# A fused attention and gated-feed-forward block on one core: K products behind the first group's h, tile 1 transposed first, bias as a full transpose

## The chip, the cores and the metric

The kernel runs on one core of one Trainium2 chip. The metric is device time in microseconds (us). A core has five engines that run their own instruction streams and wait for each other on semaphores: TensorE (PE) for matrix products, VectorE (DVE), ScalarE (ACT), GpSimd (POOL), and SyncE (SP), which here only issues DMA transfers. Products land in PSUM, eight banks of 128 x 512 float32, and have to be read out by DVE or ACT before a bank can be used again.

## The reference

The input x has 2048 tokens of 448 features, in bfloat16. All else works on its layer norm xn.

```
xn = (x - mean) / sqrt(var + 1e-5)
q, k, v = xn @ wqkv                       # 16 heads of 28
phi(t) = where(t > 0, t + 1, exp(t)) + 1e-6
kv = phi(k)^T v ;  z = sum over tokens of phi(k)
s = (phi(q) kv / (phi(q) z + 1e-6)) @ wo
h = relu(xn @ w1 + b1)^2                  # 1792 hidden features
out = x + s * silu(h @ w2 + b2)
```

## The kernel before

**Tiles and groups.** Tokens are cut into 16 tiles of 128 (`si`), four tiles to a group (`g`, 0 to 3). The 448 features are contracted in three chunks of 128 rows and a remainder of 64 rows. The hidden features of h are 14 blocks of 128 (`fi`), named H0 to H13. Per group there are three Q products of 512 tokens (Q0 to Q2), per tile one K product (K0 to K15, 448 columns). v is never formed; its weights are folded in later.

**Who sets the order.** Every step is recorded by `add` as an operation of an engine, with the tiles that it reads and writes, an estimated cost and sometimes a priority. `Program.place` then runs a model of the chip. The streams of PE and SP keep the order in which the steps are written. ACT, DVE and POOL take, among what is ready, the operation that the model wants first; some operations may go to either of two engines (`alts`), and the model chooses. Each product's buffer (`Buf`) gets the PSUM bank that the model sees free first. `Program.emit` writes out the streams with the waits that follow from all this; an operation's waits stand ahead of its first instruction. A written order on PE is therefore kept exactly, and every other engine's order, the choice of engine and the banks may move when one line moves.

**The start, tiles 0 to 3.** SP issues the loads of x and of the weights one after another. `ln_stats`, `ln_rstd` and `ln_norm` make the layer norm of a tile: DVE takes the statistics (L418, L421), ACT the root by Ln and Exp (L426, L430), DVE writes xn (L436). `ln_twin` (L448) copies the 64 features of the remainder beside themselves, since they are used from both halves of the rows. `warm` feeds PE products of ones until data is there. `tile_transpose` transposes three chunks of a tile on PE (L479) into two banks and copies them out to `xT` on ACT or DVE (L487). The first six h blocks of group 0, `heads`, are built while tiles come in: `h_part(si, c)` (L1007) adds chunk c of tile si to all six banks as one operation of six products; `h_rests` (L1022) closes them with the 64-row remainder. `b1_rows` turns the bias of h, loaded as 14 rows of 128, into columns by a transpose on PE (L1038) and a copy on ACT.

**Bursts.** After that PE works mostly in bursts of four products (`fours`), named by a text such as "Q0 Q1|Q2 H3'"; a prime means the next group. The two products left of the bar begin in the lower 64 rows of the array, the two on the right in the upper, at the same time; a burst is four operations: the first four steps of the first left and first right product, the same for the second two, and then the last three steps of each. Each operation waits for its banks as a whole.

**Evictions.** An h block is emptied by a relu with bias (L603 on ACT; two of the heads go to DVE, L600) and squared in SBUF (DVE L609 or ACT L610). A K or Q product goes through `phi`: ACT writes its exponential (L539), DVE takes min(e, 1) + 1e-6 in SBUF (L544), and then the larger of that and the product plus one, reading PSUM (L549). Only this last one sets the bank free. For each K after the first, POOL then adds the tile's result into `zacc` (L573).

**Later.** Groups 1 to 3 get their layer norm in `ln_group`, and xT by a DMA transpose that SP issues for two tiles at a time (L464). `gates` multiplies h by w2 for two tiles (L874), with a burst of the next group between its halves. The end brings the sum over tokens, the denominator, and out.

Of the kernel before, what the change touches and what calls it, by code (L numbers as in the profile page):

```python
# [9 lines left out]
P = 128  # L10
S, D, F = 2048, 448, 1792
NT, NG, NF = S // 128, S // 512, F // 128
# [24 lines left out]
class Program:  # L37
# [9 lines left out]
    def add(self, eng, emit, reads=(), writes=(), dur=0.2, alts=(), nbytes=0, mode=None, after=(), prio=None, lead=0.0):  # L47
        op = Op(eng, emit, reads, writes, {eng: dur, **dict(alts)}, mode, nbytes, after)
        for t in op.reads:
            w = self.writer.get(t)  # L50
            if w is not None:
                op.deps.add(w)
            self.readers.setdefault(t, []).append(op)
        for t in op.writes:
            w = self.writer.get(t)
            if w is not None and w is not op:
                op.deps.add(w)
            for r in self.readers.get(t, ()):
                if r is not op:
                    op.deps.add(r)  # L60
            self.writer[t] = op
            self.readers[t] = [r for r in self.readers.get(t, ()) if r is op]
        op.deps.discard(op)
        for d in op.deps:
            d.succ.append(op)
        op.prio, op.lead = prio, lead
        self.ops.append(op)
        return op
# [174 lines left out]
def bass_recurrent_scan__linear_attn_block__dense_activation_squared_relu__prompt_kernel(  # L243
    nc, A_x, A_wqkv, A_wo, B_x, B_w1, B_b1, B_w2, B_b2, out
):
    with ExitStack() as es:
        sb = lambda name, shape, dtype: es.enter_context(nc.sbuf_tensor(name, shape, dtype))
# [14 lines left out]
        w_1 = sb("w_1", [P, 4, F], bf)  # L262
        w_2 = sb("w_2", [P, NF, D], bf)
        w_o = sb("w_o", [P, 7, D], bf)
        b1r = sb("b1r", [NF, P], bf)
        b1f = sb("b1f", [P, NF], f32)
        b2b = sb("b2b", [P, D], bf)
        st6 = sb("st6", [P, NT, 6], f32)
# [28 lines left out]
        def pool(fn, writes, reads=(), dur=0.25, prio=None):  # L297
            return add("pool", fn, reads, writes, dur, prio=prio)

        pool(lambda e, _: e.memset(ident[:, :], 0.0), ["ident"], dur=0.14, prio=-9)  # L300
        pool(
            lambda e, _: e.affine_select(
# [39 lines left out]
        def dma(eng, dst, src, writes, nbytes, reads=(), after=(), prio=None, rate=None):  # L342
            return add(
                eng, lambda e, _: e.dma_start(dst, src), reads, writes, 0.45 if eng == "sp" else 0.5, nbytes=nbytes,  # L344
                after=after, prio=prio, mode=rate or 270e3,
            )

        def load_x(lo, hi, rate=None):
            dma(
                "sp", x_tok[:, lo:hi, :], x_r[:, lo // 4, lo % 4 : lo % 4 + hi - lo, :], [("x", i) for i in range(lo, hi)], (hi - lo) * P * D * 2,  # L350
                rate=rate,
            )

        def load_main(w, src, name, lo, hi):
            dma(
                "sp", w[:, 0:3, lo:hi], src[0:384, lo:hi].rearrange("(c p) j -> p c j", p=P), [(name, "m")],
                768 * (hi - lo),
            )
# [8 lines left out]
                rate=rate,  # L367
            )

        dma("act", b1r[:, :], B_b1.rearrange("(f p) -> f p", p=P), ["b1r"], F * 2, prio=-8.5)  # L370
        load_x(0, 1)
        load_x(1, 2, rate=250e3)
        load_x(2, 4, rate=300e3)
# [6 lines left out]
        for h in (0, 1):  # L380
            src = B_w1[384:448, 768:1792].rearrange("p (b j) -> p b j", j=256)[:, h::2, :]
            dst = w_1[HALF[h], 3, 768:1792].rearrange("p (b j) -> p b j", j=256)[:, h::2, :]
            dma("sp", dst, src, [("w1r", h)], 128 * 512)
        load_main(w_1, B_w1, "w1c", 1280, 1792)
        load_x(4, 8)
        load_main(w_qkv, A_wqkv, "wk", D, 2 * D)
        load_rest("sp", w_qkv, A_wqkv, "wqk", 0, 0, 2 * D)
        load_rest("sp", w_qkv, A_wqkv, "wqk", 1, 0, 2 * D)
# [27 lines left out]
        def ln_stats(si, prio=None, after=()):  # L416
            add(
                "dve", lambda e, _: e.bn_stats(st6[:, si, :], x_tok[:, si, :]), [("x", si)], [("st", si)], 0.53 if prio is None else 0.63,  # L418
                prio=prio, after=after,
            )  # L420
            add("dve", lambda e, _: e.bn_aggr(mv[:, si, :], st6[:, si, :]), [("st", si)], [("mv", si)], 0.07, prio=prio and (0.0, 0.3, 0.3, -0.5, 2.7)[prio])  # L421

        def ln_rstd(lo, hi, prio=None):
            c = slice(lo, hi)
            add(
                "act", lambda e, _: e.activation(out=rstd[:, c], in_=mv[:, c, 1], func=AF.Ln, bias=eps5[:, 0:1]),  # L426
                [("mv", i) for i in range(lo, hi)] + ["eps5", "actw"], [("ve", i) for i in range(lo, hi)], 0.19, prio=prio,
            )
            add(
                "act", lambda e, _: e.activation(out=rstd[:, c], in_=rstd[:, c], func=AF.Exp, scale=-0.5),  # L430
                [("ve", i) for i in range(lo, hi)], [("rstd", i) for i in range(lo, hi)], 0.13, prio=prio,
            )

        def ln_norm(si, prio=None):
            def norm(e, dst, src):
                return e.tensor_scalar(  # L436
                    out=dst, in0=src, scalar1=mv[:, si, 0:1], scalar2=rstd[:, si : si + 1], op0=ALU.subtract, op1=ALU.mult
                )

            return add(  # L440
                "dve", lambda e, _: norm(e, xn[:, si, 0:D], x_tok[:, si, :]), [("x", si), ("mv", si), ("rstd", si)],
                [("xn", si)], 0.3, prio=prio,
            )
# [28 lines left out]
        def pe_transpose(pieces, names, dst, name, alts, prio):  # L472

            b = Buf("T")

            def f(e, _):
                v = ps(b)[:, :].bitcast(bf)
                for k, (si, c) in enumerate(pieces):
                    last = e.transpose(v[:, k * P : (k + 1) * P], xn[:, si, c * P : (c + 1) * P], ident[:, :])  # L479
                return last  # L480

            n = len(pieces)
            add("pe", f, names + ["ident"], [b], n * 0.056, mode="128")

            def ev(e, eng):
                src = ps(b)[:, 0 : n * 64].bitcast(bf).rearrange("p (c k) -> p c k", k=P)
                return e.tensor_copy(dst, src) if eng == "dve" else e.activation(out=dst, in_=src, func=AF.Copy)  # L487

            costs = {"dve": 0.075 + n * 0.067, "act": 0.08 + n * 0.11}
            add(alts[0], ev, [b], [name], costs[alts[0]], alts=[(x, costs[x]) for x in alts[1:]], prio=prio)  # L490

        def tile_transpose(si):
            pe_transpose([(si, 0)], [("xn", si)], xT[:, si, 0:1, :], ("xT", si, 0), ("act", "dve")[: 1 + (si != 1)], 0)
            pe_transpose([(si, 1), (si, 2)], [("xn", si)], xT[:, si, 1:3, :], ("xT", si, 1), ("act", "dve")[: 1 + (si != 1)], 0.2)


        def burst(lower, upper, n):
# [484 lines left out]
        def warm(n, after=(), cols=512):  # L982
            b = Buf("W")

            def f(e, _):
                for _i in range(n):
                    last = e.matmul(ps(b)[:, 0:cols], one[:, 0:P], one[:, 0:cols], start=True, stop=True)
                return last

            add("pe", f, list(after), [b], n * cols / 1280, mode="128")  # L990

        normed = []
        for si in range(4):
            ln_stats(si, 1 + si, normed[1:2] if si == 3 else ())
            ln_rstd(si, si + 1, 0)
            normed.append(ln_norm(si, 0.6 + si))
        ln_twin(0, 3, 6)
        ln_twin(3, 4, 5)

# [34 lines left out]
        def b1_rows():  # L1034
            b = Buf("B1")
            add(
                "pe",
                lambda e, _: e.transpose(ps(b)[:, 0 : NF // 2].bitcast(bf), b1r[:, :], ident[0:NF, 0:NF]),  # L1038
                ["b1r", "ident"], [b], 0.06, mode="128",
            )  # L1040
            add(
                "act",
                lambda e, _: e.activation(out=b1f[:, :], in_=ps(b)[:, 0 : NF // 2].bitcast(bf), func=AF.Copy), [b],
                ["b1f"], 0.15, prio=0.1,
            )
# [2 lines left out]
        warm(2, [("mv", 0)], P)  # L1048
        warm(3, [("rstd", 0)], P)
        tile_transpose(0)  # L1050
        warm(2, cols=P)
        h_part(0, 0)
        tile_transpose(1)
        h_part(0, 1)
        h_part(1, 0, 1)
        tile_transpose(2)
        h_part(0, 2)
        h_part(1, 2)
        h_part(2, 0)
        tile_transpose(3)  # L1060
        h_part(2, 1)
        pe_transpose([(si, 3) for si in range(4)], [("xd", si) for si in range(4)], xT[:, 0:4, 3, :], "xT3", ("act",), 0)
        h_part(2, 2)
        h_part(3, 0)
        b1_rows()
        h_part(3, 1, 2)
# [5 lines left out]
        load_x(8, 12)  # L1072
        late_loads()
        fours("H6 H7|H8 H9", 0)
        fours("H10 K0|H12 K2", 0)
        fours("H11 K1|H13 K3", 0)
        ln_group(2)
        fours("Q0 Q1|Q2 H3'", 0)
        fours("K4 H0|K5 H4", 1)
        fours("H1 Q0|H5 Q1", 1)  # L1080
        g01 = gates(0, 1, lambda: fours("H6 H7|H9 H12", 1))
        ln_group(3)
# [69 lines left out]
```

## Time and profile before

| | us |
|---|---|
| Median of 3 runs (143.82 to 144.12) | 143.88 |
| The profiled execution | 143.73 |
| Its span, first to last instruction | 141.7 |
| PE busy | 137.3 (97%) |
| DVE busy | 90.6 (64%) |
| ACT busy | 78.9 (56%) |
| POOL busy | 27.0 (19%) |

The granted TensorE clock was 1.00 throughout. About 2 us of an execution lie outside the span of its instructions. Busy shares are means over the whole span; DVE and ACT are near full from 12 to 29 us and much less so later. In timeline rows the first number is the start, the second how long the group of like instructions lasted, then come engine, line and operation with its output and inputs. In rows of the chain, start, length and what it was.

### The profile page before, as it was taken

What the parts mean: (1) busy time and instruction counts of PE and PEld (TensorE: products, weight loads), DVE (VectorE), ACT (ScalarE), POOL (GpSimd) and SP (SyncE); (2) the same over time, 40 slices, a digit from 0 to 9 for tenths busy, and PEclk for the clock granted to TensorE, in tenths of its full rate; (3) what the DMA queues carried; (4) which work ended last, traced back from release to release, by engine and by line L of the source; (5) the groups of instructions that cost most, each with busy time, mean ns of one, the idle gap of its engine ahead of it and who ended that gap; (6) DMA issues with size and microseconds to landing.
All of it is one profiled execution on the core that took longest, in us unless ns stands there. A gap on an engine that the chain in (4) does not pass through costs nothing.

```text
span 141.7 us, 3283 instructions
## 1 busy us (share of the span) xinstructions
PE 137.3 (97%) x1343; PEld 74.9 (53%) x1343; DVE 90.6 (64%) x221; ACT 78.9 (56%) x155; POOL 27.0 (19%) x46
## 2 busy tenths in 40 slices
PE   7899999999999999999999999999999999999992
PEld 2495455555555555555556554445544555554561
DVE  1937999999886373545445879500348919277963
ACT  3727999996617283825608999474189420303020
POOL 7200014250001405005000670000000005050520
PEclk9999999999999999999999999999999999999999
DMA  4899579991733000000000000014991001203242
GB/s 103 268 287 312 187 143 297 309 307 48 122 74 74 5 0 0 5 0 0 0 5 0 0 2 5 0 37 129 175 180 39 7 0 32 97 6 128 66 136 58
DMA packets 17986, 12.90 MB, mean 91 GB/s; under 512 B 7492, under 2 KB 17588, under 8 KB 17972
## 3 DMA queue, kind: packets, MB, share of 16 engines
q1 hardware_dynamic: 16868, 11.75, 29.8%
q10 hardware_dynamic: 1104, 0.95, 3.6%
q8 instruction: 10, 0.16, 0.5%
q14 instruction: 4, 0.03, 0.1%
HBM read 9.16 MB, written 1.97 MB: 79 GB/s over the span
## 4 chain that ended last, share of the span: by engine, by line
PE 93%; DMA 3%; SPq 1%; issue 0%; DVE 0%; ACT 0%
PE pb L621 27%; PE pb L874 26%; PE pb L561 7%; PE pb L683 7%; PE pb L585 6%; PE pb L944 6%; PE pb L897 4%; PE pb L1007 3%; DMA w<-in_B_w_dram 3%; PE pb L971 1%; PE pb L657 1%; SPq L344 1%; PE pb L688 1%; PE pb L814 1%; PE pb L734 1%; PE pb L839 1%
## 5 line engine op out<-in xcount | busy, mean ns | idle before, releaser
L621 PE MATMUL pb<-xT,w 64*128 64x512 bf16 x350 | 46.5, 376 | 0.0
L603 ACT ACTIVATE r<-pb,b1f 128x512 bf16<-128x512 f32 x54 | 35.1, 693 | 18.5 <-PE pb L621 17.4
L874 PE MATMUL pb<-w,r 64*128 64x448 bf16 x392 | 39.0, 349 | 0.0
L621 PEld LDWEIGHTS pb<-xT,w 64*128 64x128 bf16 x350 | 20.6, 94 | 17.4
L874 PEld LDWEIGHTS pb<-w,r 64*128 64x128 bf16 x392 | 20.7, 94 | 16.8 <-PE pb L839 0.4
L609 DVE TENSOR_TENSOR r<-r 128x512 bf16<-128x512 bf16 x38 | 17.4, 474 | 19.0 <-ACT r L603 18.8
L573 POOL TENSOR_TENSOR zacc<-zacc,pk 128x448 f32<-128x448 f32 x13 | 13.6, 1048 | 47.9 <-DVE pk L549 47.5
L861 ACT ACTIVATE gbuf<-gbuf 128x448 bf16<-128x448 bf16 x15 | 8.1, 579 | 22.2 <-DVE gbuf L855 20.2
L933 POOL TENSOR_TENSOR gbuf<-gbuf,x_tok 128x448 bf16<-128x448 bf16 x7 | 7.2, 1031 | 44.1 <-DVE gbuf L929 44.0
L561 PE MATMUL pb<-w_qkv,xT 64*128 64x448 bf16 x112 | 14.8, 349 | 0.2 <-issue 0.2
L929 DVE TENSOR_TENSOR gbuf<-pb,gbuf 128x448 bf16<-128x448 f32 (+2 forms) x17 | 9.2, 591 | 9.0 <-PE pb L944 7.5
L585 PE MATMUL pb<-xT,w_qkv 64*128 64x512 bf16 x84 | 14.3, 376 | 0.0
L418 DVE BATCH_NORM_STATS2 st<-x_tok 128x6 f32<-128x448 bf16 x16 | 9.5, 613 | 3.0 <-DMA x_tok<-in_A_x_dram 2.9
L610 ACT ACTIVATE r<-r 128x512 bf16<-128x512 bf16 x18 | 11.0, 639 | 0.2
L549 DVE SCALAR_TENSOR_TENSOR pk<-pb,pk 128x448 bf16<-128x448 f32 x16 | 9.5, 618 | 0.2
L561 PEld LDWEIGHTS pb<-w_qkv,xT 64*128 64x128 bf16 x112 | 6.7, 94 | 5.3 <-ACT r L603 0.7
L683 PE MATMUL pb<-pk,xn 128*128 128x448 bf16 x48 | 9.4, 353 | 0.0
L855 DVE TENSOR_TENSOR gbuf<-pb,b2b 128x448 bf16<-128x448 f32 x15 | 8.7, 616 | 1.1 <-PE pb L874 0.6
L944 PE MATMUL pb<-msb,pqT 64*128 64x448 bf16 x72 | 8.3, 349 | 0.0
L549 DVE SCALAR_TENSOR_TENSOR pqT<-pb,pqT 128x512 bf16<-128x512 f32 x12 | 8.1, 687 | 0.3
L539 ACT ACTIVATE pk<-pb 128x448 bf16<-128x448 f32 x16 | 7.9, 543 | 0.5 <-PE pb L621 0.5
L585 PEld LDWEIGHTS pb<-xT,w_qkv 64*128 64x128 bf16 x84 | 5.8, 94 | 4.3 <-DVE pqT L549 0.2
(81 smaller groups left out, 119.1 us busy)
## 6 DMA issues: line engine op xcount, KB each, us to landing
out_dram<-gbuf SPq DMA_DIRECT2D x15, 112.0 KB, 1.8
x_tok<-in_A_x_dram SPq DMA_DIRECT2D x3, 448.0 KB, 8.2
w_qkv<-in_A_wqkv_dram SPq DMA_DIRECT2D x3, 336.0 KB, 7.1
w<-in_B_w_dram SPq DMA_DIRECT2D x1, 1008.0 KB, 6.0
w<-in_B_w_dram SPq DMA_DIRECT2D x2, 384.0 KB, 4.6
w_o<-in_A_wo_dram SPq DMA_DIRECT2D x1, 672.0 KB, 10.4
r<-rden_scratch SPq DMA_DIRECT2D x6, 112.0 KB
w<-in_B_w_dram SPq DMA_DIRECT2D x3, 192.0 KB, 3.8
```

Of the source, the lines that this page charges most:

```text
L418: "dve", lambda e, _: e.bn_stats(st6[:, si, :], x_tok[:, si, :]), [("x", si)], [("st", si)], 0.53 if prio is None else 0.63,
L549: lambda e, _: e.scalar_tensor_tensor(out=slot, in0=ps(buf)[:, 0:n], scalar=1.0 + 1e-6, in1=slot, op0=ALU.add, op1=ALU.max),
L561: return e.matmul(ps(b)[:, 0:D], xT[rows, si, c, :], w_qkv[rows, c, D : 2 * D], start=start, stop=stop)
L573: return e.tensor_tensor(out=o[:, dst : dst + n], in0=first[:, src : src + n], in1=pk[:, si, src : src + n], op=ALU.add)
L585: return e.matmul(ps(b)[:, 0:512].rearrange("p (s t) -> p s t", s=4), w_qkv[rows, c, m * P : (m + 1) * P], xT[rows, 4 * g : 4 * g + 4, c, ...
L603: return e.activation(out=slot, in_=ps(b)[:, 0:512], func=AF.Relu, bias=b1f[:, fi : fi + 1])
L609: return e.tensor_tensor(out=slot, in0=slot, in1=slot, op=ALU.mult)
L610: return e.activation(out=slot, in_=slot, func=AF.Square)
L621: return e.matmul(ps(b)[:, 0:512].rearrange("p (s t) -> p s t", t=P), w_1[rows, c, fi * P : (fi + 1) * P], xT[rows, ts, c, :], start=start ...
L683: last = e.matmul(ps(b)[:, 0:D], xn[:, si, c * P : (c + 1) * P], pk[:, si, :], start=(si == 0), stop=(si == NT - 1),)
L874: last = e.matmul(ps(b)[:, 0:D], r2[si // 4][HALF[h], fi, t], w_2[HALF[h], fi, :], start=(part == 0 and fi == 0), stop=(part == 1 and fi = ...
L944: return e.matmul(ps(b)[:, 0:D], ap[c][rows, :], msb[rows, c, :], start=start, stop=stop)
```

## The change

It has five parts. In the burst order of group 0 the K products of tiles 0 to 3 leave their bursts with H10 to H13 and form a burst of their own behind all h blocks of the group; K4 takes the place of H3' beside Q0 to Q2, and H3 of group 1 that of K4 in the next burst. Tile 1 is transposed ahead of the first `h_part`, the `h_part`s of tiles 0 and 1 alternate by chunk, one more product of ones stands ahead of them, tile 0's copies go to ACT alone, and the bias transpose comes one `h_part` earlier. The statistics of tiles 2 and 3 wait for the root of tile 1, where before those of tile 3 alone waited for the norm of tile 1. The load of x for tiles 4 to 7 is issued ahead of the last 512 columns of w1. The bias tile gets 128 rows, zeroed by POOL ahead of its load, and is transposed whole.

```diff
-        b1r = sb("b1r", [NF, P], bf)
+        b1r = sb("b1r", [P, P], bf)
...
+        pool(lambda e, _: e.memset(b1r[:, :], 0.0), ["b1r"], dur=0.14, prio=-9.5)
         pool(lambda e, _: e.memset(ident[:, :], 0.0), ["ident"], dur=0.14, prio=-9)
...
-        dma("act", b1r[:, :], B_b1.rearrange("(f p) -> f p", p=P), ["b1r"], F * 2, prio=-8.5)
+        dma("act", b1r[0:NF, :], B_b1.rearrange("(f p) -> f p", p=P), ["b1r"], F * 2, prio=-8.5)
...
+        load_x(4, 8)
         load_main(w_1, B_w1, "w1c", 1280, 1792)
-        load_x(4, 8)
...
         def ln_rstd(lo, hi, prio=None):
...
-            add(
+            return add(
...
         def tile_transpose(si):
-            pe_transpose([(si, 0)], ..., ("act", "dve")[: 1 + (si != 1)], 0)
-            pe_transpose([(si, 1), (si, 2)], ..., ("act", "dve")[: 1 + (si != 1)], 0.2)
+            pe_transpose([(si, 0)], ..., ("act", "dve")[: 1 + (si > 1)], 0)
+            pe_transpose([(si, 1), (si, 2)], ..., ("act", "dve")[: 1 + (si > 1)], 0.2)
...
-        normed = []
+        roots = []
         for si in range(4):
-            ln_stats(si, 1 + si, normed[1:2] if si == 3 else ())
-            ln_rstd(si, si + 1, 0)
-            normed.append(ln_norm(si, 0.6 + si))
+            ln_stats(si, 1 + si, roots[1:2])
+            roots.append(ln_rstd(si, si + 1, 0))
+            ln_norm(si, 0.6 + si)
...
-                lambda e, _: e.transpose(ps(b)[:, 0 : NF // 2].bitcast(bf), b1r[:, :], ident[0:NF, 0:NF]),
+                "pe", lambda e, _: e.transpose(ps(b)[:, 0 : P // 2].bitcast(bf), b1r[:, :], ident[:, :]),
...
         tile_transpose(0)
-        warm(2, cols=P)
+        warm(3, cols=P)
+        tile_transpose(1)
         h_part(0, 0)
-        tile_transpose(1)
+        h_part(1, 0)
         h_part(0, 1)
-        h_part(1, 0, 1)
+        h_part(1, 1)
+        h_part(0, 2)
         tile_transpose(2)
-        h_part(0, 2)
         h_part(1, 2)
-        h_part(2, 0)
+        h_part(2, 0, 1)
         tile_transpose(3)
-        h_part(2, 1)
+        h_part(2, 2)
         pe_transpose([(si, 3) for si in range(4)], ...)
-        h_part(2, 2)
         h_part(3, 0)
         b1_rows()
         h_part(3, 1, 2)
         h_rests()
...
         fours("H6 H7|H8 H9", 0)
-        fours("H10 K0|H12 K2", 0)
-        fours("H11 K1|H13 K3", 0)
+        fours("H10 H11|H12 H13", 0)
+        fours("K0 K1|K2 K3", 0)
         ln_group(2)
-        fours("Q0 Q1|Q2 H3'", 0)
-        fours("K4 H0|K5 H4", 1)
+        fours("Q0 Q1|Q2 K4", 0)
+        fours("K5 H0|H3 H4", 1)
         fours("H1 Q0|H5 Q1", 1)
         g01 = gates(0, 1, lambda: fours("H6 H7|H9 H12", 1))
```

More of the change, by code (lines that the diff above doesn't have):

```diff
@@ L492, in tile_transpose @@
         def tile_transpose(si):
-            pe_transpose([(si, 0)], [("xn", si)], xT[:, si, 0:1, :], ("xT", si, 0), ("act", "dve")[: 1 + (si != 1)], 0)
-            pe_transpose([(si, 1), (si, 2)], [("xn", si)], xT[:, si, 1:3, :], ("xT", si, 1), ("act", "dve")[: 1 + (si != 1)], 0.2)
+            pe_transpose([(si, 0)], [("xn", si)], xT[:, si, 0:1, :], ("xT", si, 0), ("act", "dve")[: 1 + (si > 1)], 0)
+            pe_transpose([(si, 1), (si, 2)], [("xn", si)], xT[:, si, 1:3, :], ("xT", si, 1), ("act", "dve")[: 1 + (si > 1)], 0.2)
         def burst(lower, upper, n):
@@ L1036, in b1_rows @@
             add(
-                "pe",
-                lambda e, _: e.transpose(ps(b)[:, 0 : NF // 2].bitcast(bf), b1r[:, :], ident[0:NF, 0:NF]),
-                ["b1r", "ident"], [b], 0.06, mode="128",
+                "pe", lambda e, _: e.transpose(ps(b)[:, 0 : P // 2].bitcast(bf), b1r[:, :], ident[:, :]),
+                ["b1r", "ident"], [b], 0.056, mode="128",
             )
```

## The prediction

> **What bounds the kernel now.** I read the page first: busy times and the chain that ended last.
>
> ```profile
> PE 137.3 (97%) x1343; PEld 74.9 (53%) x1343; DVE 90.6 (64%) x221; ACT 78.9 (56%) x155; POOL 27.0 (19%) x46
> ...
> PE 93%; DMA 3%; SPq 1%; issue 0%; DVE 0%; ACT 0%
> ```
>
> TensorE (PE) sets the end. Anything taken out of its stream, or put in, is the change of the time, unless a later wait gives it back. So I read the chain in order of time, for the places where PE stands.
>
> ```profile
> 2.68 3.77 DMA w<-in_B_w_dram
> ...
> 6.49 1.18 PE pb L1007 x18
> ...
> 15.81 0.19 issue
> 16.00 0.93 PE pb L561 x8
> ```
>
> Two places: PE waits for the second rows of w_1 until 6.49, and stands before the first K at 16.00. The pairs of 64-row matmuls before that start every 0.216 us, the last at 15.43, so the first K could have started at 15.65: the gap is 0.35 us, not 0.19. The waits view names a relu of ACT for it ("PEld pb L561 <- ACT r L603", 0.7), but the last head relu had ended at 13.96. The second half of the 64-row remainder of the Q and K weights (112 KB, issued at 8.87) fits: the DMA table gives 6.5 us to landing as the median of these two pieces, hence about 15.4 or a little later, and no other operand of K is that late.
>
> Then the timeline of the start:
>
> ```profile
> 4.67 0.61 DVE L418 BATCH_NORM_STATS2 st<-x_tok 128x6 f32<-128x448 bf16 x1
> 5.42 0.36 DVE L436 TENSOR_SCALAR xn<-x_tok,mv,rstd 128x448 bf16<-128x448 bf16 x1
> 5.84 0.34 PE L479 MATMUL pb<-ident,xn 128*128 128x128 bf16 x3
> 6.49 1.18 PE L1007 MATMUL pb<-xT,w 128*128 128x128 bf16 x18 [0.31 <-DMA w<-in_B_w_dram]
> 10.22 0.18 PE L1038 MATMUL pb<-ident,b1r 14*128 14x14 bf16 x1
> ```
>
> Last, who is next when PE comes earlier. The stretch from 22 to 29 us (windows view), then VectorE (DVE), GpSimd (POOL) and PE in it (timelines):
>
> ```profile
> 22.00:29.00 7.00, 7.00 (x70) 3.66 (x67) 6.82 (x18) 6.97 (x15) 2.74 (x3) 1.00 1.01 316
> ```
>
> ```profile
> 20.80 1.25 DVE L609 TENSOR_TENSOR r<-r 128x512 bf16<-128x512 bf16 x1
> ...
> 22.95 0.62 DVE L549 SCALAR_TENSOR_TENSOR pk<-pb,pk 128x448 bf16<-128x448 f32 x1
> 23.79 0.62 DVE L549 SCALAR_TENSOR_TENSOR pk<-pb,pk 128x448 bf16<-128x448 f32 x1
> 24.36 0.47 DVE L544 TENSOR_SCALAR pqT<-pqT 128x512 bf16<-128x512 bf16 x1
> 26.07 1.27 DVE L549 SCALAR_TENSOR_TENSOR pqT<-pb,pqT 128x512 bf16<-128x512 f32 x2
> 27.27 0.45 DVE L544 TENSOR_SCALAR pk<-pk 128x448 bf16<-128x448 bf16 x2
> ```
>
> ```profile
> 20.64 1.14 POOL L573 TENSOR_TENSOR zacc<-pk 128x448 f32<-128x448 bf16 x1 [16.01 <-DVE pk L549]
> 23.65 2.15 POOL L573 TENSOR_TENSOR zacc<-zacc,pk 128x448 f32<-128x448 f32 x2 [1.88 <-DVE pk L549]
> ```
>
> ```profile
> 23.83 0.94 PE L561 MATMUL pb<-w_qkv,xT 64*128 64x448 bf16 x8
> 24.59 1.04 PE L621 MATMUL pb<-xT,w 64*128 64x512 bf16 x8
> 27.53 0.83 PE L585 MATMUL pb<-xT,w_qkv 64*128 64x512 bf16 x6
> ```
>
> DVE and ACT are as full as PE there (6.82 and 6.97 of 7.00). PE starts three times just after DVE's L549 has emptied the PSUM bank it takes: 23.83 after 23.57, 24.59 after 24.41, 27.53 after 27.34. PE has 0.2 us of room there; a larger lead is worth something only if DVE is earlier too. And DVE's work on SBUF alone stands still while POOL adds into zacc: the square at 20.80 took 1.25 us where the median is 0.42, and ended 0.28 after POOL's 21.78; an L544 at 24.36 took 0.47 for 0.28, another at 25.48 the same. The L549, which read PSUM, keep 0.62 to 0.69 beside POOL.
>
> **The start.** Tile 1 is transposed ahead of the first h. The statistics of tile 2 now wait for rstd of tile 1, so the norm of tile 1 no longer stands behind them: ACT's exp ended at 5.00, the norm starts at 5.07 instead of 5.42, its transpose at 5.52 instead of 5.84, ACT's copy of it ends at 6.05. The first h waits longer than before: the planner gives the heads the two banks of tile 0's transpose, so it needs both copies (second one done at 5.63) and starts at 5.70, not 5.41. Then h of tile 1 at 6.11 to 6.45. The w_1 rows land as before, so at 6.49 one h part of 6 x 0.056 = 0.335 more is behind PE. Statistics of tiles 2 and 3 come later: the norm of tile 2 ends at about 7.20, and its transpose is due at 7.50; the h that follows it waits some 0.04 for the copy. Gain 0.30.
>
> **The bias.** The 14-row transpose starts 0.151 after the matmul before it and the next matmul 0.110 after that: 0.261 for two steps that otherwise take 0.056 each. As a 128-row transpose it is one more of the kind at 9.22 (0.056 apart): gain 0.15. The added memset (as ident's, 0.20) delays the identity from 1.53 to about 1.73, needed at 4.81; the bias load on ACT's queue now waits for it, and behind it ACT has nothing until 3.75. No cost. So the heads' relus start 0.45 to 0.48 earlier (11.54 to 11.06).
>
> **The order of loads.** x of tiles 4 to 7 goes ahead of the last w_1 columns on SP. At the 300 GB/s of the page those 448 KB put w_1c back by 1.5 us: issued at 6.69 with 4.6 us to landing, it comes near 12.8, and H10 to H13 want it at 14.3. x comes 1.3 us earlier, which DVE needs: it read tile 4 at 12.86 and wants to at 12.36. No cost.
>
> **K behind h.** K0 to K3 start at 17.3, after the landing near 15.9: the 0.35 is gone. The counts of matmuls are the same; Q1 with K4, and K5 with H3, pair 512 with 448 columns, but each half of the rows has 21 of the one and 7 of the other over both bursts, so at most one pair's 0.03 is lost. K4 needs only the first DMA transpose (issued at 16.12, 2.9 us). Lead of PE now 0.30 + 0.15 + 0.35 = 0.80.
>
> **What DVE makes of it.** The built program shows its order. Of the 14 squares of group 0 DVE now has 12 instead of 9 (ACT 2 instead of 5), all ahead of the first K; the K and Q evictions come in pairs (two L544, two L549). PE's last bank wait there is that of Q0 and Q1 of group 1 (at 27.53 before): their banks now come from Q1 and K4 of the burst before. Before, DVE had finished the same set, short of K4, at 27.34. Starting earlier: -0.48. Three squares at 0.335 start to start: +1.01. K4's L544 and L549: 0.19 + 0.53 = +0.72. Pairing: 0.71 each (27.27 to 28.70 for two) instead of 0.84 (22.65 to 23.49), five times: -0.6. That gives 28.0 with POOL's hold-ups as before, 0.83 + 0.19 + 0.20 = 1.22.
>
> These are the unknown. By hand: K's first L544 at 18.74 - 0.48 + 7 x 0.335 = 20.61; L549 of K0 ends at 22.15, and POOL starts 0.08 behind it (20.55 to 20.64 before), at 22.23. DVE's second L544 of the next pair would start at 22.25: held until POOL ends at 23.3, **0.9**. L549 of K3 ends at 23.97, POOL adds from 24.05 to 25.08; L544 of Q2, due at 24.43, is held, **0.5**. The L544 behind it would start 0.07 after POOL's end, the third add 0.08 after it: I take DVE first, as at 78.56 where an L544 and an add started together and the L544 kept its 0.28. Sum 1.4, so K4's bank is free at 28.2. PE starts there 0.05 later, against 27.53 before: **0.7 us later than before**, all of the lead gone (a first stop at H0 and H3, for K1's bank, comes at 23.7 to 24.6). After that PE's stream is the same, and the waits before had room of over 1.4 us at the next gates.
>
> [...]
>
> **Rivals.** (1) The third add wins its tie: another 0.9 for the L544 of Q0, +1.6, 145.5. For it: after the square of 83.47, held by one add, the next add held the L544 behind it (0.39). Chance 0.25. (2) At 22.25 DVE is first: that hold falls away and one of 0.83 remains on Q0; K4's bank at 27.6, +0.15, 144.0. Against it: POOL was ahead at 20.64 in the same place. Chance 0.22. (3) The other side: POOL holds nothing that counts, because DVE runs earlier than I make it or the adds fall beside L549s. Then K4's bank is free at 26.8, where PE comes at 27.53 - 0.80 = 26.73: a stall of 0.1 and the lead stays, -0.7, 143.2. It decides from a total of hold-ups below about 0.4. Against it: all of three L544 or squares met by an add before were held. Chance 0.17. That the K gap is not a landing, and stays, would cost 0.35 of a lead that is lost anyway.
>
> **The numbers.** The profiled execution took 143.73, its span 141.7; the median of the runs is 143.88. The forecast, chance 0.36, is span 142.4, this execution 144.4, and 144.6 on the median; its own range is 144.3 to 144.9. The range of 8 in 10 takes in rivals 1 and 2 and leaves out 3: 143.6 to 145.6. Within 0.2% (0.29 us, about what a measurement can tell) lies most of rival 2: 0.15. Faster: rival 3 and the low end of 2, 0.18. Slower: 0.67.
>
> **What would show it.** Right: h rests (L1022) near 10.6 instead of 11.1; no gap before the first K, at 17.3; PE waits for "DVE pk L549" near 24 and again near 27 to 28, 1.5 us or so together; an L544 on pk of 1.1 to 1.2 us at 22.3 beside a POOL add. Wrong: if DVE's L544 keep 0.28 between 22 and 26, or PE has no stop there; then the gain of 0.7 stands. Q0 and Q1 of group 1 start at 28.2 by my forecast, 29.1 by rival 1, 27.7 by rival 2, 26.8 by rival 3.

## The result, and the profile after

The changed kernel takes 144.16 us (median of 20 runs, 143.94 to 144.93) against 143.80 for the one before (20 runs beside it): a ratio of 1.0029, 95% interval 1.0017 to 1.0041. It is slower, by 0.36 us (0.3%), where the forecast had 0.7. The profiled execution took 144.15, with a span of 142.1.

The page after, busy times and the chain that ended last (line numbers from L300 to about L1035 are one higher than before):

```profile
PE 137.8 (97%) x1344; PEld 71.4 (50%) x1344; DVE 91.5 (64%) x224; ACT 77.3 (54%) x152; POOL 27.3 (19%) x47
...
PE 83%; DVE 12%; DMA 2%; issue 1%; SPq 0%; ACT 0%
```

The chain gave DVE nothing before (PE 93%). Now it holds 12% of the span. Where that lies is told by the chain in order of time (start, us, what):

```profile
11.22 0.34 PE pb L1023 x2
11.56 0.02 issue
11.58 0.25 DVE r L601
...
12.99 1.06 DVE st L419 x2
...
18.12 3.02 DVE r L610 x9
21.14 0.37 DVE pk L545 x2
21.50 1.06 DVE pk L550 x2
...
24.00 1.24 DVE pqT L545 x2
...
27.43 0.54 DVE pk L550
27.97 0.05 issue
28.02 1.04 PE pb L586 x8
```

From the head relus to Q0 and Q1 of group 1 at 28.02 the chain is DVE's work: statistics, nine squares, K and Q evictions, with under 0.6 us between them in which it waited for nothing that the profile shows (0.42 of it at 11.83). The waits between 22 and 29 us name the two stops of PE (engine, line, releaser: us, times, longest):

```profile
PEld pb L586 <- DVE pk L550: 1.0, 1, 1.0
...
PE pb L586 <- DVE pk L550: 0.5, 1, 0.5
PEld pb L622 <- DVE pqT L550: 0.5, 1, 0.5
```

And the same stretch in the windows view (PE, PEld, DVE, ACT, POOL busy):

```profile
22.00:29.00 7.00, 6.52 (x62) 3.79 (x60) 6.92 (x17) 5.60 (x11) 4.36 (x4) 1.00 0.97 314
```

PE was busy for 7.00 of 7.00 there before, now for 6.52; ACT, which was as full, has 1.4 us to spare; DVE, at 6.92, has next to none. Timelines of DVE and POOL:

```profile
22.48 0.46 DVE L545 TENSOR_SCALAR pk<-pk 128x448 bf16<-128x448 bf16 x2
22.85 1.15 DVE L550 SCALAR_TENSOR_TENSOR pk<-pb,pk 128x448 bf16<-128x448 f32 x2
23.91 1.33 DVE L545 TENSOR_SCALAR pqT<-pqT 128x512 bf16<-128x512 bf16 x2
25.17 1.27 DVE L550 SCALAR_TENSOR_TENSOR pqT<-pb,pqT 128x512 bf16<-128x512 f32 x2
26.36 0.28 DVE L545 TENSOR_SCALAR pqT<-pqT 128x512 bf16<-128x512 bf16 x1
```

```profile
22.66 1.17 POOL L574 TENSOR_TENSOR zacc<-pk 128x448 f32<-128x448 bf16 x1 [17.89 <-DVE pk L550]
23.91 2.30 POOL L574 TENSOR_TENSOR zacc<-zacc,pk 128x448 f32<-128x448 f32 x2
```

The pair of L545 at 22.48, whose second the forecast had held for 0.9, takes 0.46 for both: not held. Of the pair at 23.91 the second is held (1.33 for both, where the pairs without an add take 0.57 to 0.58), and no other: one hold-up by an add of POOL, as in rival 2.

The start is late. DVE waits for x tile 1 (first line, DVE's timeline), and PE begins the rests at 11.15, about where the kernel before did (11.11), and not at 10.62 (the other lines, PE's timeline):

```profile
4.09 0.63 DVE L419 BATCH_NORM_STATS2 st<-x_tok 128x6 f32<-128x448 bf16 x1 [0.31 <-DMA x_tok<-in_A_x_dram]
```

```profile
6.25 1.92 PE L1008 MATMUL pb<-xT,w 128*128 128x128 bf16 x30
...
10.33 0.22 PE L1038 MATMUL pb<-ident,b1r 128*128 128x128 bf16 x1
...
11.15 0.82 PE L1023 MATMUL pb<-xT,w 64*128 64x512 bf16 x6
11.81 6.21 PE L622 MATMUL pb<-xT,w 64*128 64x512 bf16 x56
17.85 2.81 PE L562 MATMUL pb<-w_qkv,xT 64*128 64x448 bf16 x28
```

K follows the h at 17.85 without a gap, and the bias transpose no longer spreads its neighbours. So the loss is not one thing: the lead never came in this execution, and DVE took 0.44 more than before from the rests to Q0 and Q1.

### The profile page after: what moved, and what is told of

The parts are those of the page before. It is cut to its first block, busy times and chain, and to the rows that moved or that the text cites. A ratio compares the mean times of both kernels' runs of the same rounds, so it can differ in the third digit from the quotient of the medians.

```text
span 142.1 us, 3283 instructions
## 1 busy us (share of the span) xinstructions
PE 137.8 (97%) x1344; PEld 71.4 (50%) x1344; DVE 91.5 (64%) x224; ACT 77.3 (54%) x152; POOL 27.3 (19%) x47
## 4 chain that ended last, share of the span: by engine, by line
PE 83%; DVE 12%; DMA 2%; issue 1%; SPq 0%; ACT 0%
PE pb L875 26%; PE pb L622 20%; PE pb L684 7%; PE pb L945 6%; PE pb L586 5%; PE pb L562 5%; PE pb L898 4%; PE pb L1008 3%; DVE r L610 3%; DMA x_tok<-in_A_x_dram 2%; DVE st L419 2%; DVE pk L550 2%; PE pb L972 1%; DVE pqT L550 1%; PE pb L658 1%; PE pb L689 1%
## 5 line engine op out<-in xcount | busy, mean ns | idle before, releaser
L622 PE MATMUL pb<-xT,w 64*128 64x512 bf16 x350 | 45.3, 376 | 0.0
L604 ACT ACTIVATE r<-pb,b1f 128x512 bf16<-128x512 f32 x54 | 34.4, 689 | 19.5 <-PE pb L622 18.6
L622 PEld LDWEIGHTS pb<-xT,w 64*128 64x128 bf16 x350 | 19.1, 94 | 19.4 <-DVE pqT L550 0.5
L875 PEld LDWEIGHTS pb<-w,r 64*128 64x128 bf16 x392 | 19.0, 94 | 18.4 <-PE pb L840 0.4
L862 ACT ACTIVATE gbuf<-gbuf 128x448 bf16<-128x448 bf16 x15 | 8.1, 579 | 22.0 <-DVE gbuf L856 20.2
L562 PE MATMUL pb<-w_qkv,xT 64*128 64x448 bf16 x112 | 15.5, 349 | 0.0
L550 DVE SCALAR_TENSOR_TENSOR pk<-pb,pk 128x448 bf16<-128x448 f32 x16 | 9.4, 619 | 0.1
L611 ACT ACTIVATE r<-r 128x512 bf16<-128x512 bf16 x15 | 9.2, 632 | 0.2
L550 DVE SCALAR_TENSOR_TENSOR pqT<-pb,pqT 128x512 bf16<-128x512 f32 x12 | 8.2, 688 | 0.3
```

What stands on the lines that cost most here:

```text
L550: lambda e, _: e.scalar_tensor_tensor(out=slot, in0=ps(buf)[:, 0:n], scalar=1.0 + 1e-6, in1=slot, op0=ALU.add, op1=ALU.max),
L562: return e.matmul(ps(b)[:, 0:D], xT[rows, si, c, :], w_qkv[rows, c, D : 2 * D], start=start, stop=stop)
L604: return e.activation(out=slot, in_=ps(b)[:, 0:512], func=AF.Relu, bias=b1f[:, fi : fi + 1])
L611: return e.activation(out=slot, in_=slot, func=AF.Square)
L622: return e.matmul(ps(b)[:, 0:512].rearrange("p (s t) -> p s t", t=P), w_1[rows, c, fi * P : (fi + 1) * P], xT[rows, ts, c, :], start=start ...
L875: last = e.matmul(ps(b)[:, 0:D], r2[si // 4][HALF[h], fi, t], w_2[HALF[h], fi, :], start=(part == 0 and fi == 0), stop=(part == 1 and fi = ...
```

## The experiments

Every time can be put together from three parts: when the first h rest starts, how long from there to Q0 and Q1 of group 1, and what follows. The last part is 114.12 to 114.14 us in all fourteen profiled executions, of whatever kernel. So two columns of this table explain the span. The column w_1 is the landing of the third of its three loads of rows, which decides part of the first. The ratio is of the medians of all runs; the columns behind it are of each kernel's one profiled execution, which need not be a typical one.

| kernel | ratio to before, 95% | w_1 | first rest | rest to Q0, Q1 | span |
|---|---|---|---|---|---|
| before | 1 | 6.94 | 11.11 | 16.42 | 141.7 |
| whole change | 1.0029 (1.0017 to 1.0041) | 7.61 | 11.15 | 16.86 | 142.1 |
| whole change, again | 1.0042 (1.0023 to 1.0061) | 7.71 | 11.25 | 16.86 | 142.2 |
| burst order alone | 1.0069 (1.0049 to 1.009) | 7.71 | 11.19 | 16.86 | 142.2 |
| burst order alone, again | 1.0033 (1.0008 to 1.0058) | 7.92 | 11.41 | 17.44 | 143.0 |
| all but the burst order | 0.9996 (0.9979 to 1.0013) | 7.32 | 10.86 | 16.58 | 141.6 |
| without POOL's adds | 0.9994 (0.998 to 1.0008) | 7.46 | 11.01 | 16.11 | 141.3 |
| K0 to K3 behind h only | 0.9997 (0.9975 to 1.0019) | 8.14 | 11.68 | 16.51 | 142.3 |
| squares as before | 1.0008 (0.9988 to 1.0028) | 6.94 | 10.67 | 16.79 | 141.6 |
| adds late | 1.0011 (0.9989 to 1.0034) | 7.01 | 10.68 | 16.11 | 140.9 |
| K0 to K3 only, adds late | 1.0046 (1.0026 to 1.0065) | 6.98 | 10.66 | 16.39 | 141.2 |
| adds late, four memsets | 0.9979 (0.9965 to 0.9994) | 8.05 | 11.59 | 16.11 | 141.8 |
| the same, again | 0.9977 (0.9952 to 1.0002) | 8.27 | 11.81 | 16.11 | 142.1 |
| the same on the old start | 0.9987 (0.9962 to 1.0013) | 7.82 | 11.39 | 16.11 | 141.6 |

The theory at this point (A): the burst order costs, through DVE and one hold-up by POOL; the late start was an accident. The rival (B): the new start is itself late.

**The whole change again**, with no edit.

> The changed kernel once more, unchanged, for a second profiled execution. The first one had its h rests at 11.16 instead of the forecast 10.62, because one piece of x tile 1 landed at 4.07 (before: 3.36) and the norms of tiles 0 and 1 came 0.5 late. Theory A (that lateness is an accident of one landing; the loss comes from the burst order and DVE): tile 1 lands near 3.4, the rests start at 10.6 to 10.7, and Q0 and Q1 of group 1 start near 27.7 with one DVE hold, or near 28.2 with two. Theory B (the new start is itself late, every time): the rests at 11.1 to 11.2 again, tile 1 again landing after 4.0, Q0 and Q1 near 28.0. Time by both 143.9 to 144.3, ratio to before 1.002 to 1.004.

The rests came at 11.25, Q0 and Q1 at 28.11. That is B's number, but not B's reason: x tile 1 landed at 3.53, and the third w_1 rows at 7.71. Undecided by itself; with the next ones it is not B but a landing.

**The burst order alone**, on the kernel before.

```
-        fours("H10 K0|H12 K2", 0)
-        fours("H11 K1|H13 K3", 0)
+        fours("H10 H11|H12 H13", 0)
+        fours("K0 K1|K2 K3", 0)
         ln_group(2)
-        fours("Q0 Q1|Q2 H3'", 0)
-        fours("K4 H0|K5 H4", 1)
+        fours("Q0 Q1|Q2 K4", 0)
+        fours("K5 H0|H3 H4", 1)
```

> The kernel before with the new burst order alone (four lines); start, loads and bias as before. Theory A: PE's lead of 0.45 from start and bias is absent, so K to Q run later by that, and DVE's squares and hold-ups come in full: Q0 and Q1 of group 1 start at 28.0 (one hold) to 28.7 (two), span 142.2 to 142.9, ratio 1.003 to 1.008, that is slower than the whole change or equal to it. Theory B: the bursts cost nothing or gain the 0.35 of K's gap, span 141.3 to 141.7, ratio 0.997 to 1.000.

A: 16.86 with one hold-up, 1.0069. These four lines alone make the kernel slower. On the same chip the whole change has 1.0042; the two intervals overlap, so that the four lines alone are worse than the whole is not shown.

**All but the burst order**: the same four lines, back to before, in the changed kernel.

> The changed kernel with the burst order of before (four lines back); new start, loads and bias stay. Theory A: the rests at 10.6 to 10.7, but the first K still waits for its weights until 15.9 (the gap before it grows from 0.35 to 0.8), or, if these land earlier, PE waits for K's banks at 23 to 25; no gain: span 141.6 to 141.8, ratio 0.998 to 1.000. Theory B: the start is late, rests at 11.1, span 141.9 to 142.2, ratio 1.002 to 1.004, the whole loss.

A again: 0.9996. The rests came 0.25 earlier than before, and PE then stood before the first K (timeline of PE):

```profile
15.92 0.93 PE L562 MATMUL pb<-w_qkv,xT 64*128 64x448 bf16 x8 [0.35 <-DMA w_qkv<-in_A_wqkv_dram]
```

The second half of the 64-row weights landed at 15.83 here and at 15.91 before. The gap before K is that landing, as the prediction worked out, and the old order gives any lead back there.

**Without POOL's adds** of K tiles 0 to 5: the kernel leaves these tiles out of the sum over tokens.

```
-                summed.append(si)
+                if si > 5:
+                    summed.append(si)
                 if len(summed) > 1:
-                    two, end = len(summed) == 2, len(summed) == NT
+                    two, end = len(summed) == 2, len(summed) == NT - 6
```

> The changed kernel without POOL's adds of K tiles 0 to 5 into zacc (they are left out of the column sums). Theory A: no DVE operation between 22 and 27 is held; the L545 keep 0.28; K4's bank is free 0.8 (one hold) to 1.4 (two) earlier, Q0 and Q1 of group 1 start at 26.8 to 27.3 (by how late the start is), span 141.1 to 141.6: ratio to before 0.995 to 0.999. A rival (the squares and DVE's sheer load set the end, the hold-ups lie beside other waits): Q0 and Q1 still near 28.0 and ratio 1.002 to 1.004, as with the adds.

DVE's timeline, the same operations as above:

```profile
22.34 0.46 DVE L545 TENSOR_SCALAR pk<-pk 128x448 bf16<-128x448 bf16 x2
...
23.77 0.58 DVE L545 TENSOR_SCALAR pqT<-pqT 128x512 bf16<-128x512 bf16 x2
24.26 1.28 DVE L550 SCALAR_TENSOR_TENSOR pqT<-pb,pqT 128x512 bf16<-128x512 f32 x2
```

1.33 has become 0.58, and the way from the rest to Q0 and Q1 16.11 instead of 16.86: the hold-up costs 0.75, all of it on the path. Without it the new order is 0.31 shorter than the old one (16.42). The rival, that the load of DVE alone makes the loss, falls.

**K0 to K3 behind the h only.**

```
-        fours("Q0 Q1|Q2 K4", 0)
-        fours("K5 H0|H3 H4", 1)
+        fours("Q0 Q1|Q2 H3'", 0)
+        fours("K4 H0|K5 H4", 1)
```

> The changed kernel with only K0 to K3 behind the h; K4 and h3 of the next group back in their places of before (the last two of the four lines). The measure is the time from the first h rest to Q0 and Q1 of group 1, which no landing of the start moves: 16.42 in the kernel before, 16.86 in three executions with the whole new order, 16.11 without POOL's adds, about 16.05 if PE never stops. If K4 as last product matters (the bank that Q0 and Q1 take then hangs on one more pair of DVE operations, 0.5 to 0.6): 16.3 to 16.4, ratio to before 0.997 to 1.000. If K4's place is nothing and the hold-up and the squares are all: 16.8 to 16.9, ratio 1.002 to 1.004. If here both L545 after K2 and K3 are held: about 17.0.

16.51, above the 16.3 to 16.4 of the first case, for a reason that no case had. Waits between 21 and 23 us:

```profile
PEld pb L586 <- DMA xT<-xn: 0.8, 1, 0.8
PE pb L586 <- DMA xT<-xn: 0.3, 1, 0.3
```

H3' multiplies tiles 4 to 7, whose second DMA transpose landed at 22.27; PE's gap there was 0.64 where 0.21 is the usual pitch. One L545 was held for 0.67 as well, and that did not add: the 16.11 without adds plus 0.43 for the transposes is already 16.54. So K4 in that place keeps from PE a wait for the transposes; in exchange it puts one more pair of DVE operations ahead of Q0 and Q1's banks.

**The squares as before**: five of group 0 fixed to ACT.

```
-            add("dve", square, [("r2", g, fi)], [("r2", g, fi)], 0.31, alts=[("act", 0.5)])
+            on_act = g == 0 and fi in (0, 6, 8, 11, 13)
+            add("act" if on_act else "dve", square, [("r2", g, fi)], [("r2", g, fi)], 0.5 if on_act else 0.31, alts=[("act", 0.5)] if g else [])
```

> The changed kernel with the group-0 squares shared out as before: those of h 0, 6, 8, 11, 13 fixed to ACT (5), 9 on DVE. If the three more squares on DVE set K4's bank, as the sum of the prediction had it (1.01 us): first h rest to Q0 and Q1 of group 1 falls from 16.86 to 15.9 to 16.1, PE stops nowhere, ratio 0.996 to 0.999. If ACT then gives it back (its exps of Q and K4 stand behind two more squares each): 16.6 to 16.8, ratio 1.001 to 1.003.

16.79: three squares fewer on DVE bring 0.07, not 1.01. DVE's timeline shows what took their place:

```profile
20.23 0.28 DVE L545 TENSOR_SCALAR pk<-pk 128x448 bf16<-128x448 bf16 x1 [0.59 <-ACT pk L540]
20.67 0.28 DVE L545 TENSOR_SCALAR pk<-pk 128x448 bf16<-128x448 bf16 x1 [0.16 <-ACT pk L540]
```

The L545 now wait 0.75 for ACT's exps. DVE was full, but ACT came next, 0.07 behind: with K behind all h, every relu stands ahead of the first K exp. The squares moved to ACT are not what made it late: its first K exp starts 8.99 behind the first rest here and in the changed kernel alike.

**POOL's adds late**, kept, but behind K and Q of the group.

```
+                        if si < 6:
+                            held.append((f, [("pk", si), name], [out], d))
+                        else:
+                            add("pool", f, [("pk", si), name], [out], d)
...
         fours("K5 H0|H3 H4", 1)
+        for f, reads, writes, d in held:
+            add("pool", f, reads, writes, d, after=[pr.writer["st", 8]])
```

> The changed kernel with POOL's five adds of group 0 kept, but made to wait for the statistics of tile 8 (DVE reaches them at about 28), behind K and Q of the group. If the hold-up by POOL is what costs: no L545 between 22 and 27 above 0.30, first h rest to Q0 and Q1 of group 1 16.1 as without the adds, span 141.2 to 141.5, ratio to before 0.995 to 0.999; hold-ups of 0.2 to 0.9 come after 30, where PE has room. If they cost there too, PE shows stops between 30 and 40 that it does not have in the kernel without the adds, and the ratio is 1.000 to 1.005.

In the profile the first case, to the digit: 16.11, span 140.9, the adds from 29.11, no new stop of PE. The time did not follow: 143.65 for this execution, 2.73 more than the span, where the eight profiled executions so far had 2.00 to 2.19 more, and a ratio of 1.0011.

**Both**: K0 to K3 only, and the adds late (the two edits above together).

> Both: K0 to K3 behind the h, K4 and h3 as before, POOL's adds of group 0 late. If both theories hold, PE has no stop from the h rests to 35: first h rest to Q0 and Q1 of group 1 16.05, span 130.2 to 130.3 behind the rests: 141.1 to 141.4, ratio to before 0.995 to 0.998, the fastest of all. If only the hold-up counts: as the kernel with the adds late and the whole new order, 16.1, the two equal within 0.1 us.

16.39: H3' waited again (a gap of 0.52, the transposes landed at 21.13). With the adds late, K4 as last product is the better order of the two by 0.28 (16.11 and 16.39). Outside the span lay 2.59 here.

**Four memsets more**: the late adds need four waits fewer on POOL. In both kernels with late adds the last fetches of code (8 KB each, in the trace's DMA records) start 1.04 and 2.41 behind the span, in the others one starts at 1.93 to 1.96 (burst order alone, again: none, and 1.73 outside the span); and the fetch at about 84 us that the kernels with 71 or 72 recorded POOL instructions have is missing.

```
-        pool(lambda e, _: e.memset(ones[:, :], 1.0), ["ones"], dur=0.04, prio=40)
+        for _ in range(5):
+            pool(lambda e, _: e.memset(ones[:, :], 1.0), ["ones"], dur=0.04, prio=40)
```

> The kernel with the whole change and POOL's group-0 adds late, and with four memsets more on POOL at the start (of a tile of ones, again). Late adds need four waits fewer, so POOL had 68 recorded instructions instead of 72; that execution had a span of 140.9 but took 2.73 more than its span, where the ones with 72 took 2.00 to 2.19 more, and its last instruction fetches came at 1.04 and 2.41 behind the span instead of one at 1.94. Theory: a fetch of an 8 KB piece of POOL's code fell behind the end instead of at 84. With 72 again: one fetch behind the end, time minus span 2.0 to 2.2, and the gain of the missing hold-up shows in the time: ratio to before 0.995 to 0.998. Rival: the late adds themselves cost the time outside the span or elsewhere: ratio 1.000 to 1.003 as without the memsets, time minus span 2.5 to 2.8.

The theory: one fetch at 1.95 behind the span, one at 84.36 again, time minus span 2.10, and 0.9979. Four idle memsets took some 0.5 out of the end. That is not of one execution alone: spans are on record for every run, and time minus span is 2.41 to 2.75 in 22 of the 24 runs of the two kernels with late adds (2.19 and 2.21 in the other two), 1.73 to 2.20 in all twelve with the memsets. That late adds as such cost time outside the span is thereby excluded. That the fetch is what costs it fits all records, but nothing else was changed to test it. This version is the first that is faster than the kernel before, by 0.2%.

**The same on the old start**: the burst order alone, with late adds and memsets.

> The same, late adds and four memsets, on the start, loads and bias of before: only the burst order is of the change. It shows what the new start is worth when neither K's weights nor a hold-up take it away. By the prediction's terms (0.30 + 0.15, less where w_1 lands late) the first h rest is at 11.1 to 11.2 here, against 10.66 to 10.68 in three executions of the new start with w_1's rows on time and 10.86 to 11.68 in five with one of them late; so this kernel is 0.15 to 0.45 slower than the one with the new start, ratio to before 0.998 to 1.000. If the new start is worth nothing in the mean: the two medians within 0.1 us.

16.11 again, so nothing but the start differs; the rests came at 11.39, with w_1's third rows at 7.82. The medians are 143.62 and 143.59, so the 0.15 to 0.45 expected of the new start are not there. But the spread is not the same. The old start gave 143.54 to 143.80 in ten of its runs (one at 145.28), the new one 143.03 to 143.94. Little of that lies inside the span (141.4 to 141.9 in these ten, 141.3 to 141.8 in the twelve): the run of 143.03 has a span of 141.3 and only 1.73 outside it. So on this chip the new start is worth nothing that can be told from the spread.

**Once more, the two that were open.**

> The whole change with POOL's group-0 adds late and four memsets more, once more on another chip. The first time its profiled execution had x tile 1 landing at 4.05 and the third rows of w_1 at 8.05, and its rests at 11.59. If that was an accident: rests at 10.66 to 11.0, first h rest to Q0 and Q1 16.11 again, span 140.9 to 141.3, ratio to before 0.996 to 0.999. If these landings are late with the new start as a rule: rests after 11.1 again, ratio 0.998 to 1.000.

Rests at 11.81, and this time x tile 1 was on time (3.35). What was late was one of sixteen pieces of w_1's third rows: fifteen had landed by 6.95, the last at 8.27. PE's timeline:

```profile
5.81 1.92 PE L1013 MATMUL pb<-xT,w 128*128 128x128 bf16 x24
8.32 0.51 PE L1013 MATMUL pb<-xT,w 128*128 128x128 bf16 x6 [0.58 <-DMA w<-in_B_w_dram]
```

So it is the second case of the expectation for the rests, but the ratio of the first, 0.9977: the profiled execution was the slowest of its twelve. The interval, 0.9952 to 1.0002, just reaches 1 this time.

> The kernel before with the new burst order alone, once more. Its profiled execution had one hold-up (16.86 from the first rest to Q0 and Q1) and took 144.28, but five other runs took 144.38 to 144.92. If those have the second hold-up of the prediction (the second L544 of the K pair held, 0.65 more): an execution of 144.7 to 144.9 shows 17.5 from the first rest to Q0 and Q1 and an L544 on pk of 1.1 to 1.2. If they have late landings in the start: 16.86 again and the first rest after 11.4. Ratio to before 1.004 to 1.008.

Neither case. The execution took 144.70, with 17.44 from the first rest to Q0 and Q1 and still one hold-up (an L544 of Q1, 1.03; the L544 of both K pairs took 0.45 for two). The 0.58 above 16.86 starts at 13.81 in DVE's timeline:

```profile
13.81 0.63 DVE L418 BATCH_NORM_STATS2 st<-x_tok 128x6 f32<-128x448 bf16 x1 [0.56 <-DMA x_tok<-in_A_x_dram]
...
26.44 1.03 DVE L544 TENSOR_SCALAR pqT<-pqT 128x512 bf16<-128x512 bf16 x1
```

x of tiles 4 to 7, behind w_1's last columns on the old start, landed at 13.72 and put the whole DVE chain back; from there the chain runs through DVE to Q0 and Q1. On the old start it landed at 12.23 to 12.47 in the other three executions; with the new order of loads at 11.16 to 12.36 in ten, and DVE never waited for it.

## Why the prediction was right or wrong

The sign and the place were right: PE's lead is gone, Q0 and Q1 of group 1 start later than before, and the wait has L550 of K4 at its end. The time, 144.16, lies in the stated 143.6 to 145.6, just below the forecast's own 144.3 to 144.9. That it came so near is partly luck. Q0 and Q1 started only 0.18 earlier than forecast (28.02 for 28.2), but as two terms that were off in opposite directions: the start 0.53 later than worked out, and 0.72 less from there to Q0 and Q1 (16.86 for 28.2 - 10.62 = 17.58). What follows was right (142.4 - 28.2 = 114.2; measured 114.13).

**The start, wrong in the mean.** The arithmetic holds: with w_1's rows on time the rests start at 10.66 to 10.68 (three executions), against 10.62 forecast for start and bias together. One of them (PE's timeline, adds late; there L1012 is `h_part`, L1027 the rests):

```profile
5.52 0.34 PE L480 MATMUL pb<-ident,xn 128*128 128x128 bf16 x3 [0.20 <-DVE xn L437]
5.70 2.00 PE L1012 MATMUL pb<-xT,w 128*128 128x128 bf16 x30
7.53 0.33 PE L480 MATMUL pb<-ident,xn 128*128 128x128 bf16 x3
...
10.68 0.82 PE L1027 MATMUL pb<-xT,w 64*128 64x512 bf16 x6
```

Transpose of tile 1 at 5.52, first h at 5.70, transpose of tile 2 at 7.53: forecast 5.52, 5.70 and 7.50. The step that failed is "The w_1 rows land as before". The prediction looked at the second rows alone, wanted at 6.49; when the third are wanted, and when they land, is no term of its sum. In the one execution that it read they landed at 6.94, early enough for either order. The new order puts both h parts of tiles 0 and 1 and the third chunk of tile 0 ahead of tile 2's transpose, and wants those rows by 7.14 (in this execution that part started at 7.20, and where it had to wait it started 0.04 to 0.06 behind the landing). They came later than that in seven of the ten executions with the new start, and in all seven the first rest is the landing plus 3.54 (7.61 to 11.15, 7.32 to 10.86, 8.27 to 11.81). In the first profile two landings coincide: behind the late x tile 1 PE came to these rows at 7.61, just when they landed, so either alone would have kept the rests at 11.1. On the old start the same rows are wanted some 0.5 later: a landing at 7.71 cost it 0.08. A lead that was worked out behind one DMA had run into the next one. Theory B falls in its form, since nothing shows that the change makes the landing late: the loads are issued within 0.01 us of before, and on the old start too three of four executions had these rows at 7.71 or later. It holds in its effect: the gain is mostly not had. Of all fourteen executions four had the rows by 7.01, and the one that the prediction read was one of them.

**The bias and K's gap, right.** The steps around the bias transpose have the usual pitch (0.056), K has no gap. The latter was the landing of the weights.

**The hold-ups, one instead of two.** The sum took 0.9 on the second L544 of a K pair and 0.5 on Q2's. Measured: 0 and 0, and 0.75 on the L545 of Q0 (the second of the pair at 23.91), which is rival 2's pattern. The step that failed is that POOL, starting at 22.23, holds DVE's second L544, due at 22.25, "until POOL ends at 23.3". That an add whose start is 0.02 ahead holds a DVE operation for its whole length is shown by no run. POOL's recorded start was ahead of DVE's by 8 to 17 ns in six executions (22.655 and 22.665 in the changed kernel), and in all six DVE was not held, but POOL's add took 1.17 or 1.18 instead of the 1.03 that it takes with nobody beside it. Where the starts lie further apart, DVE's square at 20.80 before, 0.17 behind an add, took 1.25 instead of 0.42, and the L545 at 24.20 after, 0.29 behind one, 1.05 instead of 0.29. But an L544 0.22 behind an add was not held (burst order alone, again: the L544 ahead of it started at 24.84, the add at 24.82; neither L544 was held, and the add took 1.39). Nor is all of DVE's work without PSUM held: a statistics step (L418 at 30.14 before), 0.70 behind an add of 1.03, kept its 0.59. From which lag on, and for which operations, an add holds DVE is not shown.

**The squares, right for DVE and not the price.** Three more squares do lie in DVE's chain, but moving them to ACT gives 0.07, as ACT's exps are next. The prediction named no second-latest wait behind that term.

**Rivals.** Rival 2 was the mechanism: 27.7 less 10.62 is 17.08, measured 16.86, and 144.0 was nearer than 144.6. Rival 3's floor (26.8 less 10.62 is 16.18) was shown by taking the adds away: 16.11. Rival 1 was not seen in any profile.

**Open.** Three of the twenty runs of the changed kernel took 144.7 to 144.9, and none of those has a trace; their spans, 142.7 for 142.1, put the difference inside the span, where a second hold-up or a later landing would each give it. The late adds without memsets ran in two groups (143.5 to 143.9 and 144.3 to 144.5), of which the faster has a trace. By their spans (140.9 to 141.3 and 141.7 to 142.1) these too differ inside the span and not behind it, by about as much as the late landings of the start cost elsewhere. Why the second DMA transpose takes 3.4 to 4.0 us from issue with K behind h, and 2.8 in the two executions with the old order, was not tried; an 8 KB code fetch falls beside it in the former (at 18.8 to 20.2) and not in the latter (23.1 and 23.7).

## What to carry to other kernels

When a change works a lead out from under one transfer, look up when each later transfer is wanted and how its landing spreads over executions: the lead ends at the first of them. An operation on another engine that holds up the bound one can cost most of its length on the path (0.75 for an add of 1.03 here), and nothing where the end does not wait for the engine that it holds: the late adds still held DVE, an L437 at 33.5 for 1.19 instead of 0.36, and PE did not stop. Move it before moving the work around it. And where a chain is full on one engine, name the second-latest wait before pricing a relief.

## What was not expected of the hardware

- **Code that is fetched at the end.** The trace's DMA records have fetches of 8 KB, of the kind "instruction", on one queue (q14). With four POOL instructions fewer, the fetch at 84 us was gone and one started 1.04 behind the span; 2.73 and 2.59 us lay outside the span, against 2.10 and 2.19 with the four memsets. That these fetches hold POOL's code is inferred from that. A missing fetch at 84 us costs nothing by itself: without the adds of K tiles 0 to 5 (60 instructions) it is gone too, none starts at 1.04, and 2.18 lay outside.
- **One piece of sixteen.** In four executions a single piece of w_1's third rows or of x tile 1 landed 0.7 to 1.3 us behind the last of its fifteen neighbours (x tile 1 in the changed kernel: 3.33 and 4.07; w_1 with adds late and four memsets, again: 6.95 and 8.27), and PE waited for it, behind x by way of DVE.
- **Half rate in the start.** PE's 128-column steps take 0.107 us at first and 0.056 later. The change came at 3.7 us in the execution before, at about 5.8 in the changed kernel and at 6.8 with K0 to K3 behind h, while the granted clock in the profile reads full (1.00 from 3.8 to 4.7 us in the changed kernel, where the steps took 0.107). It cost nothing that shows: rests at 10.68 with full rate from 3.8 us, at 10.66 with full rate from 5.3. The moment differs between executions of one kernel too: 5.4 and 6.7 us in the two with late adds and four memsets. What sets it is not shown.
